# Block-sparse attention feeding a gated MLP: the ninth unit's scores and the fifth pair's loads moved behind the first stage, and the weight transfers issued by GpSimd instead of ScalarE

## The chip, the cores and the metric

One core of one Trainium2 chip. The metric is the device time of one execution in microseconds (us). The engines are named as in the profile: PE is TensorE (PEld its weight loads), DVE is VectorE, ACT is ScalarE, POOL is GpSimd, SP is SyncE; "ACTq" and "SPq" are rows for transfers that the sequencers of ACT and SP issue.

## The reference, cut to what matters

```python
# attention: q, k, v are (4 batches, 8 heads, 768 rows, 64); blocks of 32 rows, 24 blocks
scores = (q @ k^T) / 8
mask   = |block_i - block_j| <= 1, or either block is the first or last,
         or block_j is one of 3 sampled blocks of block_i
attn   = softmax(where(mask, scores, -1e9)) ;  out = attn @ v
# gated MLP over the 3072 rows of 512 numbers
h = x @ w_in ;  g = h * sigmoid(1.702 * h) ;  y = g @ w_out      # w_in 512x2048, w_out 2048x512
```

All in float32; w_in and w_out come as 64-bit words whose conversion to float32 is done on the chip.

## The kernel before

**Units, pairs and chunks.** The work on attention is cut into 48 units of 64 rows (two blocks of a batch). Two units of the same rows in two batches share their loads: such a pair has one entry in `kent` (keys, `load_k`: about ten transfers on SP, 1.5 MB) and one in `vent` (values, `load_v`: one or three on SP and two gathers of 512 KB each on POOL). There are two buffers for each (`RING`), so an entry's loads can go out when the entry two before it has been used. Eight units give the 512 rows of a chunk of the MLP; there are six chunks of 16 steps `m` (one slice of 128 hidden columns each), 96 steps in all.

**One unit** goes through `scores` (32 small matmuls, then on DVE four minima, L285, and on ACT four exponentials, L297), `transposes` (8 on PE, two copies L318 on ACT), `factors`, `values` (64 small matmuls), `normalise` (L381) and `turn` (transposes, then `xhi` on ACT L399 and `xlo` on DVE L400).

**One step of the MLP**, `tick(m)`: `up` (12 matmuls, L499 to L501, float32 in three products of high and low parts), `gate` (ACT L507 and L512, DVE L514), `gate_hi` (ACT L519), `gate_lo` (DVE L527), and `down` of the step before (12 matmuls, L545 to L550).

**The weights' conversion**, `weights`, is a generator of 32 items k, one for each slice of w_in or w_out in turn (k even from 2 on is w_out). Item k is fetched (L422: 512 KB of words into `raw`, 3 buffers), then ACT L430 makes `a` (3 buffers), DVE L454, L460 and L464 finish it, ACT L467 copies its high part and DVE L435 gives the low part; for w_out the finished `a` is also stored to `ws` (L441, 256 KB) for the later chunks. The fetch of item k+2 is called at the start of item k and reuses the buffer that L464 of item k-1 has read; the store of item k-1 is called right after that. The generator stops after each few instructions and is advanced by hand: 21 advances in the first stage, then nine in a step, or six in a step in which a unit's scores are due (`tick`, `heavy`).

**What sets the order.** Every engine runs its own list in program order, and the order is written by hand: `first` (the first stage: the first nine units, one after the other, with the first five weights) and then `plan`, which gives each further unit a place on a clock of four quarters per step. In `plan`, chunk 1's units begin at quarter -4, which puts the ninth unit's scores into `first`; `begin` calls `loads` at each quarter. In `first`, `vmost` holds back all value loads but the first until the second unit's minima are done: POOL copies `nm` to `seen` (L703), and later gathers stand behind that copy in POOL's list. Transfers on SP and ACT take their landing semaphores from one set of eight in turn (`DMAHW0` to `7`), those on POOL from another (`DMASW0` to `7`); the one that takes a semaphore again waits until the transfer that had it before has landed.

## Time and profile before

| what | us |
|---|---|
| median of 3 runs (785.55 to 786.63) | 786.6 |
| the profiled execution: its own time | 786.88 |
| its span, first to last instruction | 785.1 |
| first stage, up to the first matmul of `up` | 77.43 |
| chunk 0, 16 steps | 123.0 |
| PE busy | 739.7 (94%) |
| DVE busy | 412.9 (53%) |
| ACT busy | 383.4 (49%) |
| POOL busy | 45.8 (6%) |

1.8 us of the profiled execution lie outside its span. Matmuls of one PE overlap in the records, so PE's busy time is larger than its work; the pace of PE is read from the distance between the starts of like matmuls.

### The profile page before, as it was taken

How to read it: one execution, taken by the hardware profiler on the slowest of the kernel's cores; microseconds unless marked ns; L12 is line 12 of the kernel's file. 1: busy time of each engine (PE TensorE's matmuls, PEld its weight loads, DVE VectorE, ACT ScalarE, POOL GpSimd, SP SyncE). 2: the span in 40 equal slices, each digit the busy share in tenths (PEclk: the TensorE clock that was granted, in tenths of full speed). 3: DMA queues.
4: the chain of work that ended last, by engine and by line, in shares of the span. 5: the costliest groups of instructions: out<-in, count | busy, mean ns of one | idle time of the engine just before them, and what ended most of it. 6: DMA issues, size and time to landing. Idle time of an engine off the chain costs nothing.

```text
span 785.1 us, 19231 instructions
## 1 busy us (share of the span) xinstructions
PE 739.7 (94%) x7584; PEld 571.3 (73%) x7584; DVE 412.9 (53%) x1076; ACT 383.4 (49%) x951; POOL 45.8 (6%) x67
## 2 busy tenths in 40 slices
PE   2675999999999999999999999999999999999997
PEld 2453776767777777787787787787777777788885
DVE  4465888888554444554444445445454444443333
ACT  3455667766645444454444454544455445333232
POOL 3011011011000000000000000000000000000000
PEclk9787999999999999999999999999999999999999
DMA  8997887876664256563443564544574231131111
GB/s 246 293 336 255 271 277 234 257 247 225 205 187 162 75 168 188 168 204 115 150 147 110 163 187 121 156 128 126 171 249 156 68 108 41 41 96 52 47 47 55
DMA packets 62956, 128.21 MB, mean 163 GB/s; under 512 B 7569, under 2 KB 28946, under 8 KB 62354
## 3 DMA queue, kind: packets, MB, share of 16 engines
q1 hardware_dynamic: 48802, 82.08, 34.7%
q0 software_dynamic: 6336, 23.07, 8.7%
q10 hardware_dynamic: 7728, 21.84, 8.5%
q8 instruction: 60, 0.98, 0.5%
q14 instruction: 30, 0.25, 0.1%
HBM read 116.47 MB, written 10.49 MB: 162 GB/s over the span
## 4 chain that ended last, share of the span: by engine, by line
PE 77%; DMA 7%; DVE 7%; ACT 5%; issue 2%; SPq 1%; ACTq 0%; DVEq 0%
PE bank L499 11%; PE bank L549 10%; PE bank L550 10%; PE bank L545 10%; PE bank L501 10%; PE bank L500 10%; PE bank L313 5%; PE bank L339 4%; PE bank L262 4%; DMA ws<-a 2%; DMA vmid<-in_v_dram 2%; PE bank L347 2%; PE bank L274 2%; DVE a L460 1%; ACT ex L297 1%
## 5 line engine op out<-in xcount | busy, mean ns | idle before, releaser
L499 PE MATMUL bank<-xhi,win 128*128 128x512 f32 x384 | 158.2, 412 | 0.5 <-DVE g L514 0.2
L514 DVE SCALAR_TENSOR_TENSOR g<-g,bank 128x512 f32<-128x512 f32 x83 | 57.0, 687 | 184.3 <-ACT g L507 184.3
L549 PE MATMUL bank<-wout,ghi 128*128 128x512 f32 x384 | 153.9, 401 | 0.0
L550 PE MATMUL bank<-wout,ghi 128*128 128x512 f32 x384 | 152.0, 396 | 0.0
L501 PE MATMUL bank<-xhi,win 128*128 128x512 f32 x384 | 150.8, 393 | 0.0
L500 PE MATMUL bank<-xlo,win 128*128 128x512 f32 x384 | 150.6, 392 | 0.0
L297 ACT ACTIVATE ex<-bank,nm 128x256 f32<-128x256 f32 (+1 forms) x172 | 82.8, 490 | 116.7 <-DVE nm L285 116.5
L507 ACT ACTIVATE g<-bank 128x512 f32<-128x512 f32 x96 | 57.4, 598 | 146.7 <-PE bank L501 145.4
L545 PE MATMUL bank<-wout,glo 128*128 128x512 f32 x384 | 107.7, 394 | 0.0
L488 DVE TENSOR_TENSOR wout<-wst,wout 128x512 fp32r<-128x512 f32 x80 | 55.4, 692 | 79.7 <-ACT wout L487 78.7
L285 DVE CUSTOM_DVE_ANT_1 bank<-bank,bias 128x256 f32<-128x256 f32 x176 | 73.8, 440 | 23.2 <-PE bank L262 20.2
L499 PEld LDWEIGHTS bank<-xhi,win 128*128 128x128 f32 x384 | 72.1, 188 | 19.0 <-ACT wst L512 1.3
L519 ACT CAST ghi<-g 128x512 fp32r<-128x512 f32 x96 | 59.6, 621 | 53.1 <-DVE g L514 53.1
L545 PEld LDWEIGHTS bank<-wout,glo 128*128 128x128 f32 x384 | 72.1, 188 | 17.4
L550 PEld LDWEIGHTS bank<-wout,ghi 128*128 128x128 f32 x384 | 72.2, 188 | 16.5
L549 PEld LDWEIGHTS bank<-wout,ghi 128*128 128x128 f32 x384 | 72.1, 188 | 16.4
L501 PEld LDWEIGHTS bank<-xhi,win 128*128 128x128 f32 x384 | 72.1, 188 | 16.0
L500 PEld LDWEIGHTS bank<-xlo,win 128*128 128x128 f32 x384 | 72.2, 188 | 12.8
L262 PE MATMUL bank<-kg,qt 64*32 64x256 f32 x1408 | 54.9, 408 | 22.5 <-DMA kg<-in_kb_dram 18.6
L218 POOL DMA_INDIRECT vown<-in_v_dram,vidx x44 | 43.2, 983 | 516.7 <-PE bank L339 402.0
L318 ACT COPY pt<-bank 128x512 f32<-128x512 f32 (+1 forms) x112 | 56.9, 560 | 29.8 <-PE bank L313 29.6
L527 DVE TENSOR_TENSOR glo<-g,ghi 128x512 fp32r<-128x512 f32 x96 | 65.7, 685 | 0.7 <-ACT ghi L519 0.7
(88 smaller groups left out, 809.7 us busy)
## 6 DMA issues: line engine op xcount, KB each, us to landing
wst<-ws SPq DMA_DIRECT2D x80, 256.0 KB
kg<-in_kb_dram SPq DMA_DIRECT2D x151, 128.0 KB
kg<-in_kb_dram SPq DMA_DIRECT2D x22, 384.0 KB
raw<-in_moe_w_in_dram ACTq DMA_DIRECT2D x16, 512.0 KB
raw<-in_moe_w_out_dram ACTq DMA_DIRECT2D x16, 512.0 KB
kg<-in_kT_dram SPq DMA_DIRECT2D x4, 1536.0 KB
vown<-in_vd_dram SPq DMA_DIRECT2D x8, 768.0 KB
qt<-in_q_dram SPq DMA_DIRECT2D x22, 256.0 KB
```

The source lines that it names most:

```text
L262: nc.tensor.matmul(sps[h][BLK * c:BLK * (c + 1), n * i:n * (i + 1)].rearrange("p (n s) -> p n s", s=BLK), self.qt[r][rows, bi, UT * pair + ...
L285: nc.vector.tensor_tensor_reduce(out=at, in0=at, in1=bias, scale=-SCALE, scalar=3.0e38, op0=ALU.add, op1=ALU.min, accum_out=un["nm"][:, ha ...
L297: nc.scalar.activation(out=ex, in_=sps[h][:, n * k:n * (k + 1)], func=AF.Exp, bias=un["nm"][:, half, c:c + 1], scale=-1.0, accum_out=un["r ...
L499: nc.tensor.matmul(h, wih[:, k], hi[:, k], start=(k == 0), stop=False)
L500: nc.tensor.matmul(h, wih[:, k], lo[:, k], start=False, stop=False)
L501: nc.tensor.matmul(h, wil[:, k], hi[:, k], start=False, stop=(k == NCT - 1))
L507: nc.scalar.activation(out=g, in_=self.h, func=AF.Tanh, scale=0.851)
L519: self.nc.scalar.copy(out=ghi, in_=self.g[m][0])
L527: self.nc.vector.tensor_tensor(out=glo, in0=g, in1=ghi.bitcast(F32), op=ALU.subtract)
L545: nc.tensor.matmul(o[n], glo[:, tk[n]], woh, start=False, stop=last)
L549: nc.tensor.matmul(o[n], ghi[:, tk[n]], woh, start=(f == 0), stop=False)
L550: nc.tensor.matmul(o[n], ghi[:, tk[n]], wol, start=False, stop=False)
```

## The change

Three edits. `plan` begins chunk 1 at quarter 4 instead of -4, and `first` treats eight units and not nine, so the ninth unit's scores stand in the loop, and chunk 1's eight units are spread over 52 quarters from quarter 4 on (at 4, 10, 17, 23, 30, 36, 43, 49) where seven of them stood at 4, 12, 20, 28, 36, 44, 50. `kmost` and `vmost` hold back the entries of the fifth pair and later until the eighth unit's minima: `hold` puts the copy to `seen` into POOL's list, and a small transfer from `nm` to `seen` into SP's. And the transfers L422 and L441 are issued by POOL.

```diff
-        self.vmost = 1
+        self.kmost, self.vmost = CU // 2, 1
...
-            if self.knext < len(self.kent) and (self.knext < RING or not self.kent[self.knext - RING]["scores"]):
+            if self.knext < self.kmost and (self.knext < RING or not self.kent[self.knext - RING]["scores"]):
...
-                nc.scalar.dma_start(out=raw, in_=self.w64[i][f])
+                nc.gpsimd.dma_start(out=raw, in_=self.w64[i][f])
...
-                nc.scalar.dma_start(out=self.ws[f], in_=tiles[k]["a"].bitcast(F32))
+                nc.gpsimd.dma_start(out=self.ws[f], in_=tiles[k]["a"].bitcast(F32))
...
-            begin = -4 if c == 1 else 4 * QT * (4 * c - 4) - 8
+            begin = 4 if c == 1 else 4 * QT * (4 * c - 4) - 8
...
-        nc, items = self.nc, self.items[:CU + 1]
+        nc, items = self.nc, self.items[:CU]
...
+        def hold(g, k):
+
+            nc.gpsimd.tensor_copy(out=self.seen[:, 0:NPAIR], in_=g["unit"]["nm"][:, 0])
+            self.vmost = k
+
...
             if n == 1:
-                nc.gpsimd.tensor_copy(out=self.seen[:, 0:NPAIR], in_=g["unit"]["nm"][:, 0])
-                self.vmost = len(self.vent)
+                hold(g, CU // 2)
...
+        behind = self.transposes(items[CU - 1])
+        after = self.values(items[CU - 2])
+        finish(behind[:2])
+        finish(self.turn(items[CU - 3]))
+        finish(behind[2:])
+        finish(after)
+        weights(4)
+        after = self.values(items[CU - 1])
         finish(self.turn(items[CU - 2]))
-        finish(self.values(items[CU - 1]))
+        finish(after)
+        hold(items[CU - 1], len(self.vent))
+        nc.sync.dma_start(out=self.seen[:, NPAIR:2 * NPAIR], in_=items[CU - 1]["unit"]["nm"][:, 0])
+        self.kmost = len(self.kent)
+        self.loads()
         finish(self.turn(items[CU - 1]))
-        self.loads()
```

**ACT in the first stage**, at the eighth unit. The names: `ghi` and `glo` hold a unit's exponentials, `wst` and `pt` its transposed ones; a wait's name ends in a number that is the same for all. Before:

```order
L467 CAST wout_117<-a 128x512 [waits DVE_49]
L422 DMA raw<-in_moe_w_in_dram 128x1024 [waits DMAHW2_49,Activation_49]
L441 DMA ws_69<-a 128x512 [waits DMAHW5_49]
L430 ACTIVATE a<-raw 128x512 [waits DMAHW1_49,Activation_49]
L318 COPY wst<-bank_88 128x512 [waits PE_49]
```

In the changed kernel:

```order
L467 CAST wout_117<-a 128x512 [waits DVE_49]
L430 ACTIVATE a<-raw 128x512 [waits DMASW4_49,Activation_49]
L318 COPY wst<-bank_88 128x512 [waits PE_49]
L318 COPY wst<-bank_92 128x512 [waits PE_49]
L297 ACTIVATE ghi,rs<-bank_89,nm 128x256 [waits DVE_49]
```

The two issues with their waits for earlier landings no longer stand ahead of L430; L430 itself waits for its own words alone.

**POOL's list around the end of the first stage**, as a difference (`vown_97` and `vown_98` are the two buffers of gathered values, `ws_69` to `ws_71` the stored slices):

```order
+L441 DMA ws_69<-a 128x512
+L422 DMA raw<-in_moe_w_out_dram 128x1024
+L422 DMA raw<-in_moe_w_in_dram 128x1024
+L687 COPY seen<-nm 128x4
+L218 DMA vown_97<-in_v_dram,vidx 128x1024 x2
+L218 DMA vown_98<-in_v_dram,vidx 128x1024 x2
+L441 DMA ws_70<-a 128x512
+L422 DMA raw<-in_moe_w_out_dram 128x1024
+L422 DMA raw<-in_moe_w_in_dram 128x1024
+L441 DMA ws_71<-a 128x512
```

The four gathers of the fifth and sixth pair, which were two and two with the first stage's last third between them, stand together, and between the fetch of item 7 (the `w_in` row ahead of the copy) and the store `ws_70` of item 4, with the fetches of items 8 and 9 behind.

**ACT at the first two steps of the loop** (`g`, `wst` and `ghi` are the gate's; `ex` the exponentials of the unit whose scores stand at quarter 4). Before:

```order
L512 COPY wst<-bank_92 128x512
L422 DMA raw<-in_moe_w_out_dram 128x1024 [waits DMAHW6_49]
L430 ACTIVATE a<-raw 128x512 [waits DMAHW5_49,DMAHW3_49,Activation_49]
L519 CAST ghi<-g 128x512 [waits DVE_49]
L467 CAST wout_119<-a 128x512 [waits DVE_49]
```

In the changed kernel:

```order
L512 COPY wst<-bank_92 128x512
L430 ACTIVATE a<-raw 128x512 [waits DMASW0_49,DVE_49]
L519 CAST ghi<-g 128x512 [waits DVE_49]
L467 CAST wout_119<-a 128x512 [waits DVE_49]
L297 ACTIVATE ex,rs<-bank_85,nm 128x256 [waits DVE_49,PE_49]
...
L507 ACTIVATE g<-bank_92 128x512 [waits PE_49]
L512 COPY wst<-bank_92 128x512
L430 ACTIVATE a<-raw 128x512 [waits DMASW6_49,DMASW5_49]
```

L430 of item 7 waits for one transfer (its words) where it waited for two (the words and the store `ws_70`); the second landing, `DMASW5`, is now awaited by L430 of item 8.

## Rows read from the trace of the kernel before

**Rows 1.** The busy time of each engine in four stretches (us from the span's start: the stretch, its length, then PE, PEld, DVE, ACT and POOL busy with the count of instructions, the granted clock as a share, the DMA engines' busy share and GB/s): the end of the first stage in two parts, steps 0 and 1, and steps 2 to 15.

```profile
40.77:57.30 16.53, 13.54 (x318) 9.10 (x302) 12.10 (x39) 9.96 (x30) 2.15 (x3) 0.84 1.04 340
57.30:77.43 20.13, 8.77 (x183) 6.35 (x183) 10.98 (x36) 9.55 (x29) 3.28 (x4) 0.75 0.78 250
77.43:90.20 12.77, 12.34 (x145) 9.10 (x143) 10.12 (x25) 7.86 (x20) 0.19 (x1) 1.00 0.94 311
90.20:200.45 110.25, 106.82 (x1174) 81.69 (x1175) 93.96 (x222) 75.92 (x178) 9.37 (x8) 1.00 0.76 245
```

**Rows 2.** The matmuls of L499 alone (four to a step) in chunk 0, in chunk 3 with its eight units, and in thirteen steps without attention: stretch, length, PE and PEld busy with counts, clock, DMA share, GB/s.

```profile
77.43:200.45 123.02, 26.63 (x64) 12.16 (x65) 1.00 0.78 252
446.64:562.45 115.81, 26.58 (x65) 12.21 (x65) 1.00 0.52 155
693.38:765.76 72.38, 20.47 (x53) 9.75 (x52) 1.00 0.23 62
```

**Rows 3.** The chain of waits that ended last, from 53 us on: start, length, what.

```profile
53.55 7.37 DMA vmid<-in_v_dram
60.95 0.34 ACTq L441
...
61.39 0.66 ACT a L430
62.05 0.96 ACT wst L318 x2
63.01 0.92 ACT ghi L297 x4
63.93 0.91 ACT glo L297 x4
64.84 0.27 ACT xhi L399
...
77.78 5.35 DMA ws<-a
```

**Rows 4.** ACT in order of time: start, length, engine, line, operation, tiles, count, and in brackets the idle time before it with what ended it.

```profile
45.77 0.47 ACT L297 ACTIVATE ghi<-bank,nm 128x256 f32<-128x256 f32 x1 [0.73 <-DVE nm L285]
52.56 0.47 ACT L297 ACTIVATE ghi<-bank,nm 128x256 f32<-128x256 f32 x1
61.39 0.66 ACT L430 ACTIVATE a<-raw 128x512 f32<-128x512 f32 x1 [4.32 <-DMA vmid<-in_v_dram]
62.89 0.50 ACT L297 ACTIVATE ghi<-bank,nm 128x256 f32<-128x256 f32 x1
69.76 0.47 ACT L297 ACTIVATE ghi<-bank,nm 128x256 f32<-128x256 f32 x1 [0.48 <-DVE nm L285]
71.58 0.37 ACT L399 CAST xhi<-bank 128x256 fp32r<-128x256 f32 x1
83.23 0.67 ACT L430 ACTIVATE a<-raw 128x512 f32<-128x512 f32 x1 [1.69 <-DMA ws<-a]
90.04 0.70 ACT L430 ACTIVATE a<-raw 128x512 f32<-128x512 f32 x1
121.83 0.33 ACTq L441 DMA_DIRECT2D ws<-a  x1
126.48 0.68 ACT L430 ACTIVATE a<-raw 128x512 f32<-128x512 f32 x1 [1.14 <-DMA ws<-a]
```

**Rows 5.** DVE in order of time, columns as in rows 4: the ninth unit's first minimum and the end of item 4.

```profile
68.66 0.43 DVE L285 CUSTOM_DVE_ANT_1 bank<-bank,bias 128x256 f32<-128x256 f32 x1
72.93 0.68 DVE L464 SCALAR_TENSOR_TENSOR a<-raw,a 128x512 int32<-128x512 int32 x1
160.05 0.54 DVE L454 TENSOR_SCALAR a<-a 128x512 int32<-128x512 int32 x1
```

**Rows 6.** PE: the first matmul of step 0, a unit's scores, the first of steps 1 and 2 (columns as in rows 4).

```profile
77.43 0.48 PE L499 MATMUL bank<-xhi,win 128*128 128x512 f32 x1
80.36 1.09 PE L262 MATMUL bank<-kg,qt 64*32 64x256 f32 x32
90.22 0.50 PE L499 MATMUL bank<-xhi,win 128*128 128x512 f32 x1
```

**Rows 7.** POOL's gathers (columns as in rows 4), and over all 44 of them the time from issue to landing.

```profile
75.44 0.94 POOL L218 DMA_INDIRECT vown<-in_v_dram,vidx  x1 [16.24 <-PE bank L339]
76.68 0.94 POOL L218 DMA_INDIRECT vown<-in_v_dram,vidx  x1 [0.30 <-PE bank L392]
159.23 1.11 POOL L218 DMA_INDIRECT vown<-in_v_dram,vidx  x1 [27.32 <-PE bank L339]
...
DMA to landing us min/median/max: 4.5/6.1/9.6
```

**Rows 8.** ACT's waits from 57 to 192 us (who waited for whom: total us, times, longest), and over the whole span the durations of L454 (ns min/median/max, first and last start, form).

```profile
ACT a L430 <- DMA ws<-a: 5.9, 6, 1.7
...
L454 DVE TENSOR_SCALAR a<-a x32: 396/420/537, 36.2 to 189.3; 128x512 int32<-128x512 int32 x32
```

**Rows 9.** SP's issue of a pair's key loads (columns as in rows 4).

```profile
81.58 0.35 SPq L189 DMA_DIRECT2D qt<-in_q_dram  x1
83.76 6.29 SPq L200 DMA_DIRECT2D kg<-in_kb_dram  x6
```

More of the change, by code (lines that the diff above doesn't have):

```diff
@@ L671, in first @@
     def first(self):
-        nc, items = self.nc, self.items[:CU + 1]
-        assert items[CU]["unit"]["n"] == CU
+        nc, items = self.nc, self.items[:CU]
+        assert self.items[CU]["unit"]["n"] == CU
         nc.scalar.activation(out=self.seen[:, 0:1], in_=self.zero, func=AF.Exp)
@@ L683, in weights @@
                 next(self.conv)
+        def hold(g, k):
+            nc.gpsimd.tensor_copy(out=self.seen[:, 0:NPAIR], in_=g["unit"]["nm"][:, 0])
+            self.vmost = k
         for n, g in enumerate(items):
-            behind = []
-            if n == CU:
-                behind = self.transposes(items[n - 1])
             exps = self.scores(g)
-            if 0 < n < CU:
-                behind = self.transposes(items[n - 1])
+            behind = self.transposes(items[n - 1]) if n else []
             if n > 3:
```

## The prediction, made before the changed kernel ran

> **What bounds the kernel now.** I read the busy times by stretch first, then the distances of like matmuls, then the chain of waits, then ACT, DVE and POOL in order of time around the end of the first stage. In the last 20 us of the first stage no engine is near full: PE, DVE and ACT are busy 8.8, 11.0 and 9.6 of 20.1 us [rows 1]; engines wait for each other and for landings. In chunk 0 PE and DVE are both close to full: in steps 2 to 15, 110.25 us, DVE is busy 93.96, and PE shows 106.82 [rows 1]. How much PE could give is seen from like matmuls [rows 2]: thirteen steps without attention take 72.38 us, 5.57 each; chunk 3 with its eight units takes 115.8, so a unit costs PE (115.8 - 16 x 5.57) / 8 = 3.3 us. Seven units in chunk 0 would give 112 us, and it takes 123.0. From chunk 1 on the pace is PE's and the change touches nothing there, so only two numbers matter: when chunk 0 starts, and how long it lasts.
>
> Sums are made on the profiled execution (786.88 us, of which 785.1 are its span); the median of the runs, 786.6, is 0.3 less. About 0.2% (1.6 us) is what a measurement of this kernel can tell from no change.
>
> **The first stage gets shorter: the stall.** The chain [rows 3] goes from a value load (`vmid`, 53.55 to 60.9) through ACT's issue of a store (L441 at 60.95) to L430 at 61.39. ACT does not need that load; its store takes a landing semaphore that the load had, and ACT stood idle 4.32 us for it [rows 4]. With both issues on POOL this wait is POOL's. The eighth unit's exponentials, at 62.89, would then follow the seventh's (52.56) by the distance that the seventh's kept from the sixth's (45.77), 6.79 us: at 59.35. **Gain 3.5 us.** The words of items 0 and 1 go out some 10 us sooner, since POOL's list has nothing ahead of them that waits, while the second pair's keys are landing; item 2's words then stand behind two gathers on POOL. These pull both ways; I take 0, from a loss of 2 to a gain of 1.
>
> **The first stage gets shorter: the ninth unit.** Its minima start at 68.66 and xhi follows its exponentials at 71.58 [rows 4, 5], 2.9 us on the way from the eighth unit's exponentials to step 0. They go from here; the two copies of transposes and one L430, which fill part of this time today, stay on ACT. **Gain 2.5 us** (1.5 to 3). Step 0 would begin at 77.43 - 3.5 - 2.5 = 71.4 [rows 6].
>
> **The first stall of the loop.** L430 of item 7 waits at 83.23 for a store, 1.69 us [rows 4]. In the new order it waits only for its words and for DVE; the store is awaited by L430 of item 8, one step on. I take 1.5. So step 2, which began at 90.22 [rows 6], would begin 7.5 us sooner, at 82.7.
>
> **What POOL's list gives back.** Item 4's end (L464 at 72.93 [rows 5], 0.7 long) moves up by the stall's 3.5 and some 1.8 of the ninth unit's time, to 68.3. Only then can POOL issue item 7's words, which stand ahead of the copy and of four gathers; a gather takes 0.94 and 0.30 until the next [rows 7], so from about 69.9 to 74.9, and the store `ws_70` goes out at 75, item 8's words at 76.2. A gather lands 6.1 us after its issue at the median, 9.6 at the longest [rows 7], so item 8's words are there at 82.3 to 85.8. ACT would reach item 8's L430 at 90.04 - 7.5 = 82.5 [rows 4]. A wait of 0 to 3.3 us, and a shorter one at item 9. I take **2 us**, past the median, since just then both pairs' keys, 3 MB on SP, and 3.75 MB on POOL want to move within 20 us, some 340 GB/s, which is all that a stretch shows (340 GB/s at a share of 1.04 [rows 1]). The keys themselves have time: SP needs some 8.5 us for a pair [rows 9], from about 60 on, and the scores need them only at about 74.
>
> **The unit that moves into the loop.** From step 2 on, chunk 0 holds seven units' starts where it held six. One more costs PE 3.3 us [rows 2], DVE about as much. Both engines are used as densely as now, so I scale by the 123.0 us of chunk 0 over its 112 of PE's work, which gives 3.6, and take **3.5 us** (3.0 to 4). The scores alone, 1.09 us on PE [rows 6], are not the price, because the whole chain of units moves with them.
>
> **The transfers' latency.** A store issued by ACT at 121.83 frees its buffer for L430 at 126.48 [rows 4], 4.65 us. From POOL the fetch goes first (0.94 and 0.30), and a transfer of POOL lands after 4.5 to 9.6 us, 6.1 at the median [rows 7]: 5.7 to 10.8, at the median 7.3, so 2.7 us later. That price comes from gathers of twice the bytes; the change's plain transfers have no row. L430 stands seven advances behind the L464 that makes the store possible. In a step of nine advances that is some 5.5 us, in a step of six 8 or more. In the new order the whole distance lies within or almost within a nine-advance step for items 13, 21, 27 and 31 and partly for 17; a wait of 1.8 at four and 0.9 at one is 8.1 us, against 4.2 now (5.9 less the 1.69 [rows 4, 8]). Of the 4 us more, PE loses perhaps three quarters, since ACT's gates are queued behind the waiting L430 and PE's `down` behind the gates: **3 us**, from 0 (the latency is that of ACT's) to 7 (it binds at every pair of items).
>
> A figure of the Trainium skill would make this smaller: "DMA: Bandwidth & Descriptors", section Latency and other measured facts, gives a first byte after about 0.6 us from ACT or SP and about 1 us from POOL. By that alone the term would be near 0.5 us and the sum about -1.5. The rows here, in which POOL's transfers land 1.5 us later than ACT's store at the median, speak for more.
>
> **The sum:** -3.5 - 2.5 - 1.5 + 2 + 3.5 + 3 = **+1.0 us**, 786.6 + 1.0 = **787.6 us**: what the first stage gains, the loop gives back.
>
> **The rivals.**
>
> *A: the latency hides, faster.* If POOL's plain transfers land like ACT's, the last term is 0 and the wait at item 8 shrinks to 0.5: -7.5 + 0.5 + 3.5 = -3.5, **783 us**. For it: a plain transfer needs no list of rows, and POOL issues at L464's end, without ACT's queue ahead of it. Against it: the gathers' 6.1 us.
>
> *B: the store's landing becomes the loop's clock, slower.* The place is the chain L464 - POOL's fetch - store - landing - L430, three items long, in chunk 0. It decides where that distance passes the eight advances between two odd items' L430, some 8 us. Were it 9 (7.3, and 1.5 from L430 to the next L464), each of some eleven pairs from item 9 on would be 1 us late: 11 us less the 4 that ACT waits now, +7 where I took +3; with 3 at item 8 it gives +6 to +8, **794 us**. For it: six stores already end an idle time of ACT [rows 8], with the shorter latency. Against it: there is slack in steps of six.
>
> *C: DVE and POOL lock each other out, slower.* L454 begins right when L464 ends, and so does POOL's fetch. While a gather ran from 159.23, L454 took 0.54 where it takes 0.42 [rows 5, 7, 8]: 0.12 us, for 32 items at most 4 us. If the fetch held it up for its whole 0.94 us, 27 items in chunk 0 would cost up to 25 us of a DVE that is 85% busy, half of it seen: **800 us**. The Trainium skill says something like it ("SBUF — State Buffer", section Who interferes with whom): DVE's two-port modes and GpSimd shut each other out for a whole instruction. The 0.12 us of this trace speaks against the full price.
>
> *D: the first stage does not shrink.* If the early words delay the second pair's keys, or item 2's words come late behind the gathers, the 3.5 us shrink to 1: +3.5, **790 us**.
>
> **How the numbers follow.** Forecast 0.45, A 0.27, B 0.18, C 0.04, D 0.06. The forecast's own range is 784.5 to 791. A alone is faster; of the forecast's 0.45 some 0.08 are, 0.22 lie within 0.2% and 0.15 are slower; with B, C and D: faster 0.35, same 0.22, slower 0.43. The lower end takes all terms at their favourable bounds, -8.5 + 0 + 3.2 + 0: 781. The upper is B with 3 us of D: 796. C's tail is left out.
>
> **What would show it.** Right: the first matmul of step 0 at 71 to 72.5; no idle time of ACT at the eighth unit put down to `vmid`; POOL with four gathers in a row at about 70 to 75 and `ws_70` behind them; L430 of items 8 and 9 waiting for POOL's transfers; step 2 at 82 to 85; more ACT idle time put down to `ws` in chunk 0 than 5.9 us; the rest of the kernel, from chunk 1 on, as long as before. Wrong: a chunk 0 of less than 126 us from step 0 on (then A), or of more than 134 (then B or C, told apart by whether ACT's L430 waits or DVE's L454 is longer), or a step 0 at 74 or later (D).

## The result, and the profile after

| | before | changed |
|---|---|---|
| median, us (runs) | 786.6 (785.55 to 787.7, 4) | **797.4** (796.35 to 798.36, 4) |
| span of the profiled execution | 785.1 | 794.6 |
| first matmul of step 0 | 77.43 | 70.50 |
| chunk 0 | 123.04 | 139.46 |

The ratio is 1.0137, with a 95% interval of 1.0118 to 1.0156: 10.8 us slower. 787.6 was forecast, with 796 as the upper end. In the traces the first stage is 6.9 us shorter (6.0 forecast) and chunk 0 is 16.4 us longer; from chunk 1 on nothing differs (584.6 us in both). The profiled execution of the changed kernel was the fastest of its four, so the traces hold 9.5 of the 10.8 us.

The windows of the changed kernel (columns as in [rows 1]): the end of the first stage, steps 0, 1 and 2, and steps 2 to 15.

```profile
57.30:70.50 13.20, 8.00 (x211) 5.42 (x209) 8.27 (x26) 6.84 (x20) 2.68 (x6) 0.76 0.78 232
70.50:77.18 6.68, 6.58 (x45) 4.24 (x45) 3.94 (x8) 2.26 (x5) 4.20 (x5) 0.58 0.95 304
77.18:84.41 7.23, 6.90 (x33) 5.35 (x33) 5.93 (x16) 4.63 (x13) 1.40 (x3) 1.00 1.04 400
84.41:96.34 11.93, 9.98 (x121) 6.93 (x121) 8.79 (x22) 7.49 (x19) 1.27 (x3) 0.86 0.92 281
84.41:209.96 125.55, 114.95 (x1281) 86.75 (x1281) 97.24 (x233) 78.46 (x188) 27.32 (x43) 0.97 0.76 235
```

Some of these matmuls, in order of time (columns as in [rows 6]), the first two of steps 0 and 1:

```profile
70.50 0.80 PE L499 MATMUL bank<-xhi,win 128*128 128x512 f32 x1 [0.46 <-ACT xhi L399]
71.97 0.63 PE L499 MATMUL bank<-xhi,win 128*128 128x512 f32 x1
...
77.18 0.50 PE L499 MATMUL bank<-xhi,win 128*128 128x512 f32 x1
77.97 0.39 PE L499 MATMUL bank<-xhi,win 128*128 128x512 f32 x1
```

Against [rows 1] three things are new: step 0 runs at a granted clock of 0.58, for most of it the lower of the two levels (1.2 of 2.4 GHz), so that its second L499 comes 1.47 us behind the first where step 1 takes 0.79; the transfers of step 1 take the DMA engines' whole share (1.04 at 400 GB/s, where steps 0 and 1 had 0.94 at 311); and PE, which was busy 106.8 of 110.3 us in steps 2 to 15, is busy 115.0 of 125.6.

POOL at the end of the first stage, in order of time (columns as in [rows 7]):

```profile
68.65 0.20 POOL L687 COPY seen<-nm 128x4 f32<-128x4 f32 x1
69.02 1.01 POOL L218 DMA_INDIRECT vown<-in_v_dram,vidx  x1 [0.17 <-issue]
70.33 0.97 POOL L218 DMA_INDIRECT vown<-in_v_dram,vidx  x1 [0.30 <-PE bank L392]
71.60 1.31 POOL L218 DMA_INDIRECT vown<-in_v_dram,vidx  x1 [0.30 <-DVE wout L435]
73.22 0.94 POOL L218 DMA_INDIRECT vown<-in_v_dram,vidx  x1 [0.30 <-issue]
74.16 0.60 POOL L441 DMA_DIRECT2D ws<-a  x1
74.73 0.58 POOL L422 DMA_DIRECT2D raw<-in_moe_w_out_dram  x1
```

The backlog is the one that the prediction drew: four gathers, then `ws_70`, then item 8's words. ACT in order of time (columns as in [rows 4]), the eighth unit's first exponential and then the time of step 2:

```profile
58.84 0.47 ACT L297 ACTIVATE ghi<-bank,nm 128x256 f32<-128x256 f32 x1 [0.59 <-DVE nm L285]
...
85.41 0.66 ACT L430 ACTIVATE a<-raw 128x512 f32<-128x512 f32 x1 [1.06 <-DMA raw<-in_moe_w_out_dram]
88.18 0.67 ACT L430 ACTIVATE a<-raw 128x512 f32<-128x512 f32 x1 [1.08 <-DMA ws<-a]
88.76 1.05 ACT L318 COPY pt<-bank 128x512 f32<-128x512 f32 x2
```

Items 8 and 9 wait 2.1 us together. What the prediction did not have is the last row: the copies of the ninth unit's transposes stand behind item 9's L430, and the next unit's scores wait 1.95 us for them. The waits in chunk 0 (who waited for whom: total us, times, longest), and the landings of POOL's fetches L422:

```profile
PEld bank L262 <- ACT pt L318: 13.4, 12, 4.0
PE bank L262 <- ACT pt L318: 8.7, 6, 3.6
ACT a L430 <- DMA raw<-in_moe_w_out_dram: 3.9, 5, 1.3
ACT a L430 <- DMA ws<-a: 3.9, 4, 1.2
```
```profile
DMA to landing us min/median/max: 3.7/5.0/10.6
```

L262 are a unit's scores. In the loop `psum` gives scores and transposes the same banks 0 and 1, so a unit's scores cannot begin before ACT has copied its predecessor's transposes out of them (L318). ACT's own waits for stores, which rivals A and B turned on, went down from 5.9 us [rows 8] to 3.9.

**Where the 16.4 us lie.** The length of each step, from its first matmul L499 to the next one's, in the profiled execution of each kernel (us):

| kernel | step 0 begins | 0 | 1 | 2 | 3 to 7 | 8, 9 | 10, 11 | 12 to 15 | chunk 0 |
|---|---|---|---|---|---|---|---|---|---|
| before | 77.4 | 5.0 | 7.8 | 7.8 | 38.7 | 14.5 | 15.2 | 34.1 | 123.0 |
| **changed** | 70.5 | 6.7 | 7.2 | 11.9 | 39.4 | 21.4 | 14.5 | 38.2 | 139.5 |
| e1 | 74.0 | 5.0 | 6.7 | 7.8 | 38.5 | 15.3 | 15.2 | 34.1 | 122.6 |
| e2 | 74.2 | 6.7 | 9.0 | 9.5 | 40.3 | 21.1 | 14.6 | 38.2 | 139.3 |
| e3 | 75.5 | 4.9 | 7.8 | 7.1 | 40.8 | 14.6 | 17.0 | 34.6 | 126.8 |
| e4 | 70.1 | 6.6 | 7.7 | 7.8 | 40.1 | 19.5 | 15.7 | 38.0 | 135.3 |
| e5 | 70.3 | 4.4 | 7.2 | 15.4 | 38.5 | 20.9 | 14.6 | 38.0 | 139.1 |
| e6 | 70.4 | 6.8 | 7.1 | 11.9 | 40.5 | 21.3 | 14.5 | 39.1 | 141.2 |
| e7 | 75.7 | 5.0 | 6.7 | 8.8 | 42.4 | 22.0 | 14.6 | 31.6 | 131.0 |
| e8 | 75.5 | 5.7 | 6.7 | 7.8 | 37.6 | 14.6 | 16.4 | 33.0 | 121.9 |
| e9 | 71.5 | 5.8 | 7.2 | 11.1 | 42.5 | 19.1 | 14.6 | 38.4 | 138.7 |
| e10 | 72.5 | 6.5 | 7.2 | 8.1 | 44.1 | 20.0 | 14.5 | 40.4 | 140.9 |
| e11 | 70.0 | 5.5 | 6.6 | 11.1 | 40.9 | 19.1 | 16.0 | 36.8 | 136.0 |
| e12 | 72.4 | 5.8 | 7.2 | 11.6 | 39.8 | 22.5 | 14.5 | 37.9 | 139.4 |
| e13 | 70.8 | 6.0 | 7.2 | 10.5 | 40.6 | 20.8 | 14.5 | 37.8 | 137.4 |
| e14 | 77.4 | 6.2 | 6.7 | 7.9 | 40.9 | 22.0 | 14.5 | 32.3 | 130.5 |
| e15 | 73.5 | 6.7 | 7.2 | 7.9 | 40.6 | 22.8 | 14.5 | 38.9 | 138.7 |
| e16 | 76.9 | 4.6 | 7.9 | 6.7 | 38.8 | 14.7 | 23.0 | 31.6 | 127.3 |
| e17 | 70.8 | 6.6 | 7.2 | 12.0 | 37.9 | 19.7 | 14.5 | 34.7 | 132.5 |
| e18 | 74.0 | 5.0 | 6.7 | 7.8 | 35.6 | 14.5 | 14.5 | 31.3 | 115.3 |

The changed kernel loses in step 0 (1.7), in step 2 (4.1), in steps 8 and 9 (6.9) and in 12 to 15 (4.1). Each length is that of one execution, and an execution can lie some way off its kernel's median: e4's was 3.0 us below, e10's 3.9 above.

### The profile page after: what moved, and what is told of

Its sections match the earlier page's. It is cut to its first block, busy times and chain, and to the rows that moved or that the text cites. A ratio compares the mean times of both kernels' runs of the same rounds, so it can differ in the third digit from the quotient of the medians.

```text
span 794.6 us, 19264 instructions
## 1 busy us (share of the span) xinstructions
PE 748.6 (94%) x7584; PEld 575.8 (72%) x7584; DVE 413.6 (52%) x1076; ACT 383.1 (48%) x951; POOL 72.4 (9%) x116
## 3 DMA queue, kind: packets, MB, share of 16 engines
q0 software_dynamic: 12224, 44.05, 17.3%
## 4 chain that ended last, share of the span: by engine, by line
PE 77%; DMA 7%; ACT 6%; DVE 5%; issue 3%; SPq 2%; ACTq 0%; DVEq 0%; POOLq 0%
PE bank L499 11%; PE bank L549 10%; PE bank L550 10%; PE bank L501 10%; PE bank L500 10%; PE bank L545 10%; PE bank L313 5%; PE bank L339 4%; PE bank L262 4%; DMA kg<-in_kb_dram 2%; DMA ws<-a 2%; PE bank L347 2%; PE bank L274 2%; ACT ex L297 1%; DMA raw<-in_moe_w_out_dram 1%
## 5 line engine op out<-in xcount | busy, mean ns | idle before, releaser
L499 PE MATMUL bank<-xhi,win 128*128 128x512 f32 x384 | 159.5, 415 | 2.7 <-DVE g L514 1.5
L297 ACT ACTIVATE ex<-bank,nm 128x256 f32<-128x256 f32 (+1 forms) x176 | 84.8, 491 | 122.7 <-DVE nm L285 122.4
L499 PEld LDWEIGHTS bank<-xhi,win 128*128 128x128 f32 x384 | 72.8, 190 | 22.9 <-ACT wst L512 2.7
L262 PE MATMUL bank<-kg,qt 64*32 64x256 f32 x1408 | 58.7, 415 | 27.9 <-DMA kg<-in_kb_dram 18.3
L550 PEld LDWEIGHTS bank<-wout,ghi 128*128 128x128 f32 x384 | 72.2, 188 | 16.4
L549 PEld LDWEIGHTS bank<-wout,ghi 128*128 128x128 f32 x384 | 72.1, 188 | 16.4
L318 ACT COPY pt<-bank 128x512 f32<-128x512 f32 (+1 forms) x112 | 56.8, 559 | 25.4 <-PE bank L313 25.3
```

Source lines behind the costliest of these rows:

```text
L262: nc.tensor.matmul(sps[h][BLK * c:BLK * (c + 1), n * i:n * (i + 1)].rearrange("p (n s) -> p n s", s=BLK), self.qt[r][rows, bi, UT * pair + ...
L297: nc.scalar.activation(out=ex, in_=sps[h][:, n * k:n * (k + 1)], func=AF.Exp, bias=un["nm"][:, half, c:c + 1], scale=-1.0, accum_out=un["r ...
L499: nc.tensor.matmul(h, wih[:, k], hi[:, k], start=(k == 0), stop=False)
L549: nc.tensor.matmul(o[n], ghi[:, tk[n]], woh, start=(f == 0), stop=False)
L550: nc.tensor.matmul(o[n], ghi[:, tk[n]], wol, start=False, stop=False)
```

## The experiments

e1, e2 and so on are the first parts of the runs' labels. Theory 1, formed from the waits above: the loss comes from the units' new distances. Units at 4, 12, 20, ... have four quarters of a step between one unit's transposes and the next one's scores; at 4, 10, 17, 23, ... two or three. (The kernel before has two such distances of 6 as well, after its starts at 44 and 50.) Ratios are to the kernel before, each with its 95% interval.

### Which part of the change: e1, e2

**e1**, the kernel before with the two issues on POOL alone:

```diff
-                nc.scalar.dma_start(out=raw, in_=self.w64[i][f])
+                nc.gpsimd.dma_start(out=raw, in_=self.w64[i][f])
...
-                nc.scalar.dma_start(out=self.ws[f], in_=tiles[k]["a"].bitcast(F32))
+                nc.gpsimd.dma_start(out=self.ws[f], in_=tiles[k]["a"].bitcast(F32))
```

> The kernel before with the two issues on POOL and nothing else: nine units in the first stage, chunk 1's units at quarters 4, 12, 20, 28, 36, 44, 50. Theory 1 (what chunk 0 lost comes from the eight units at distances of 6 and 7 quarters: the scores of a unit need the two PSUM banks that its predecessor's transposes fill, and must wait until ACT has copied them, L318): no such waits here beyond those of the kernel before, the stall of ACT at the eighth unit goes, step 0 starts at 73 to 74 instead of 77.4, chunk 0 lasts 121 to 124, total 782 to 784. Rival 2 (POOL's issues make the weights late all through chunk 0): chunk 0 lasts 128 or more, total 788 to 792.

784.3 us, 0.998 (0.9965 to 0.9994): **faster** than both kernels, by 2 us against the one before. Chunk 0 takes 122.55 where it took 123.04, although L430 waits 6.5 us there for stores and waited 5.7 before. The transfers' latency, +3 in the prediction, costs chunk 0 nothing.

**e2**, the changed kernel with these two lines as before:

> The changed kernel with the two issues back on ACT: the ninth unit in the loop and the fifth pair's loads held back, as changed. Theory 1 (distances of units): chunk 0 keeps nearly all of its loss, 136 to 139 us from step 0 to step 16; step 0 at 70.5 to 73, the total 796 to 800. Rival 2 (POOL's issues): chunk 0 falls back to 126 to 128, total 786 to 789. Rival 3 (POOL's backlog of four gathers ahead of the words of items 8 and 9): only step 2 gets shorter, from 11.9 to about 9, total 794 to 795.

799.95 us, 1.0169 (1.0147 to 1.0191). All of chunk 0's loss is there without POOL's issues: 139.32. Rival 2 falls; the change's two halves pull apart, -2 and +13.7 us.

### One unit more, or closer units: e3, e7

**e3**, the changed kernel with `begin = 0` in place of 4: eight starts at 0, 8, 16, 24, 32, 38, 44, 50.

> The changed kernel with chunk 1's units from quarter 0 on instead of 4: they stand at 0, 8, 16, 24, 32, 38, 44, 50, so four of the seven distances are 8 again, and three are 6, like the last two of the kernel before. Same number of units in chunk 0, same issues on POOL. Theory 1: the waits of scores for L318 at steps 2 and 8 go, chunk 0 lasts 131 to 133 instead of 139.5, total 789 to 791. Rivals 2 and 3 (POOL's transfers or its backlog): nothing changes or it gets worse, since the weights are as late as before and the work starts sooner, 796 to 799.

789.1 us, 1.0028 (1.001 to 1.0046), chunk 0 126.75, steps 2 and 8 without their loss. Its loop holds eight units' starts, and its chunk 0 is 4.2 us longer than e1's with seven. That is not the price of a unit alone: the first of the eight stands ahead of step 0's first matmul, and three of the distances are 6 where e1 has one. So it does not contradict the prediction's 3.5 us, and does not show it either.

**e7**, e1 with its seven starts closer together and nothing else:

```diff
+                if c == 1:
+                    q = (-4, 4, 10, 17, 23, 30, 36, 43)[k] - begin
                 starts.append((begin + q, g))
```

> The kernel before with the two issues on POOL, nine units in the first stage and so seven starts in the loop as before, but those seven at the distances of the changed kernel: 4, 10, 17, 23, 30, 36, 43 instead of 4, 12, 20, 28, 36, 44, 50. The work in every stage stays that of the first experiment; only the distances change. Theory 1: the scores wait for L318 at steps 2 and 8 again, chunk 0 lasts 130 to 134 where that kernel's took 122.6, total 792 to 796. Rival 5 (what chunk 0 lost is the work of one unit more, in engines that are full): chunk 0 stays at 122 to 124, total 784 to 786.

793.7 us, 1.0087 (1.0068 to 1.0107). **With the same work as e1 chunk 0 takes 131.04, 8.5 us more**; steps 8 and 9 take 22.0 where e1 takes 15.3. Rival 5 falls: the distances alone make about half of the loss.

### What happens at step 8: e4, e9, e12, e14

PE and then ACT in the changed kernel at step 8 (columns as in [rows 4] and [rows 6]):

```profile
138.49 1.16 PE L313 MATMUL bank<-ident,ex 128*128 128x128 f32 x8
141.59 1.10 PE L545 MATMUL bank<-wout,glo 128*128 128x512 f32 x4
146.28 1.58 PE L262 MATMUL bank<-kg,qt 64*32 64x256 f32 x32 [3.60 <-ACT pt L318]
```
```profile
138.83 0.62 ACT L519 CAST ghi<-g 128x512 fp32r<-128x512 f32 x1
139.34 0.69 ACT L430 ACTIVATE a<-raw 128x512 f32<-128x512 f32 x1
139.92 0.61 ACT L467 CAST wout<-a 128x512 fp32r<-128x512 f32 x1
141.12 0.68 ACT L430 ACTIVATE a<-raw 128x512 f32<-128x512 f32 x1 [0.58 <-DMA raw<-in_moe_w_out_dram]
143.05 0.62 ACT L467 CAST win<-a 128x512 fp32r<-128x512 f32 x1 [1.26 <-DVE a L464]
143.57 0.59 ACT L507 ACTIVATE g<-bank 128x512 f32<-128x512 f32 x1
144.06 0.58 ACT L512 COPY wst<-bank 128x512 f32<-128x512 f32 x1
145.09 0.67 ACT L430 ACTIVATE a<-raw 128x512 f32<-128x512 f32 x1 [0.45 <-DMA ws<-a]
145.67 1.05 ACT L318 COPY pt<-bank 128x512 f32<-128x512 f32 x2
```

The unit that starts at quarter 30 has its transposes at 34, in the third quarter of step 8. PE is through with them at 139.65, and has two quarters of work left, up to 142.7. ACT's copies stand in its list behind six advances of the weights and the gate, and come at 145.67. At the old places (scores at the first quarter of a step, transposes at the first of the next) the copies stand ahead of a step's weights, and PE has four quarters.

**e4**: transposes three quarters after the scores instead of four, so one quarter more for the copies.

```diff
-                turn = q + (4 if self.sparse(g) else 2)
+                turn = q + ((3 if q < 4 * QT * 4 - 8 else 4) if self.sparse(g) else 2)
```

> The changed kernel with the transposes of chunk 1's units three quarters after their scores instead of four, starts unchanged (4, 10, 17, ...): ACT has one quarter more (some 1.4 us of PE) for the copies before the next unit's scores want the banks. Theory 1: the scores' waits for L318 (22 us on PE and its weight loads in chunk 0) shrink by more than half, chunk 0 lasts 131 to 135, total 789 to 793; some of it comes back as waits of transposes for the exponentials L297. Rivals 2 and 3: no change, 796 to 798.

794.8 us, 1.0116 (1.0098 to 1.0135), chunk 0 135.31. Step 2 takes 7.79, what it takes in e1; step 8 still 11.5. PE's waits of scores for L318 fell from 8.7 to 1.9 us, and 3.0 came back as waits for exponentials. The median is above the expected range by 2 us.

**e9**: copies before the advances that lie behind the gate.

```diff
-            self.gate(m, lambda: run(n1))
-        finish(after[:2])
+            self.gate(m, lambda: (finish(after[:2]), run(n1)))
```

> The changed kernel with one order changed in the loop: where a unit's transposes or scores stand in the third quarter of a step, ACT's copies L318 (or exponentials L297) come before the three advances of the weights behind the gate, and so before an L430 that waits for a store to land, instead of after them. Theory 1 (the scores wait for the banks because the copies stand in ACT's list behind the weights): in step 2 the copies need not wait for item 9's L430 at 88.18, the scores' wait of 1.95 there goes and step 2 takes 8 to 9.5 instead of 11.9; in step 8, where the copies still stand behind two other items, 12 to 13 instead of 14.2; total 791 to 794. If ACT's order has no part in it (the weights themselves come late for `up` and `down`): 796 to 799.

798.5 us, 1.0157 (1.0137 to 1.0178). The expectation was wrong on step 2: the L430 of 88.18 belongs to the end of step 1's weights, and the edit does not move it. Step 8 did fall to 12.5, but steps 3 to 7 took 3.1 us more: an L430 waited 2.8 us for a store there, and PE waited 1.7 and 1.0 us for the gate's copy L512 behind it. No gain.

**e12** asks whether the shared banks carry the loss.

```diff
-..., {"s": (0, 1), "t": (0, 1), "a": (2,)}[what]
+..., {"s": (0, 1), "t": (5, 6) if k < 2 * CU else (0, 1), "a": (2,)}[what]
...
-        o = [self.bank[3 + n] for n in range(NN)]
+        o = [self.bank[3 + (n % 2 if c == 0 else n)] for n in range(NN)]
```

> The changed kernel with banks 5 and 6 for the transposes of chunk 0's units, so that scores (banks 0 and 1) never wait for the copies L318. To have the two banks, chunk 0's `down` adds the third and fourth block of tokens onto the first and second (same matmuls, same count; the results of the first 512 rows are mixed up). Theory 1 (the shared banks carry the loss): no scores wait for L318, chunk 0 falls from 139.5 to 127 to 131 us (the changed kernel from quarter 0 on took 126.8), total 785 to 789. Rival 6 (the weights' chain on ACT and DVE is the clock, the banks only show where PE waits for it): PE waits elsewhere, chunk 0 stays at 136 to 140, total 794 to 798.

799.9 us, 1.0169 (1.0148 to 1.0189), chunk 0 139.4: **theory 1 falls in the form in which the banks are the cause.** PE's waits in its chunk 0:

```profile
PE bank L339 <- DVE xlo L400: 6.4, 4, 4.3
...
PE bank L339 <- ACT pt L318: 1.8, 1, 1.8
PE bank L262 <- ACT pt L318: 1.4, 1, 1.4
```

With banks to spare the scores go ahead, and PE waits at the next row of its list, the values L339, for the same copies and for `xlo`, which follows them on ACT and DVE and frees the bank of the values. At step 8 the copies come 6.1 us behind PE's transposes, 6.0 in the changed kernel: the shared bank was only the first thing that met the late copies.

**e14**, the same two lines on e7:

> The kernel of e7 (nine units in the first stage, POOL's issues, seven starts at 4, 10, 17, 23, 30, 36, 43) with transposes in banks 5 and 6 in chunk 0 as in e12. Theory 1: the 8.5 us that the distances cost go, chunk 0 122 to 125 (e7 131.0, at distances of 8 122.6), total 784.5 to 787. Rival 6: 129 to 131, total 792 to 794.

795.5 us, 1.0111 (1.0094 to 1.0128), chunk 0 130.50, step 8 14.6: the same answer.

### Are the weights the cause: e13, e15, e16, e17, e18

**e13** leaves out the stores (`save` only drops the item, `stream` loads from `vd`).

> The changed kernel without the sixteen stores L441: later chunks load as many bytes of values instead of the stored slices, so w_out is wrong from chunk 1 on. No L430 waits for a store to land, POOL issues sixteen transfers less and 4 MB less are moved in the first 200 us. Theory 1: of the three waits of L430 that push copies (1.08, 0.45, 1.2 us) two go, chunk 0 136 to 138.5, total 794 to 796.5. Rival 6 in the form that the landing of stores is the clock of the weights' chain: chunk 0 128 to 132, total 786 to 790.

794.9 us, 1.0118 (1.0098 to 1.0138), chunk 0 137.4: two of the 16.4 us. **e15**, with e12's edit too:

> The edits of e12 and e13 together. If banks and stores each carry a part: 2 to 4 us less than e12 alone. If the banks carry all: as e12, within 1 us. If the stores do: as e13.

797.3 us, 1.0127 (1.0105 to 1.0149), chunk 0 138.7, more than with e13's edit alone: the two do not add.

**e16**: e7's edit with the starts 6, 14, 22, 30, 38, 44, 50.

> The kernel of e1 (nine units in the first stage, POOL's issues) with the seven starts at 6, 14, 22, 30, 38, 44, 50 instead of 4, 12, 20, 28, 36, 44, 50: the first five stand in the third quarter of a step instead of the first, at distances of 8. Theory 7 (ACT comes to a unit's copies some 7 us after PE's transposes when they stand in the third quarter, behind the weights and the gate; two quarters of PE's work, 2.8 us, don't cover that, four quarters, 5.6 us, nearly do): chunk 0 123 to 127, total 784 to 789. If the quarter alone makes the loss, whatever the distance: chunk 0 130 or more, total 792 or more.

788.3 us, 1.0031 (1.0013 to 1.0049). Through step 9 the transposes stand in the third quarter too, but at distances of 8, and nothing is lost (steps 8 and 9: 14.7). At 38 and 44 the distance falls to 6, the transposes are at 42, the scores at 44, and step 10 alone takes 15.65. PE and ACT there:

```profile
153.25 0.66 PE L313 MATMUL bank<-ident,ex 128*128 128x128 f32 x4 [0.26 <-ACT ex L297]
155.84 1.10 PE L545 MATMUL bank<-wout,glo 128*128 128x512 f32 x4
160.77 2.65 PE L262 MATMUL bank<-kg,qt 64*32 64x256 f32 x32 [3.83 <-ACT pt L318]
```
```profile
156.91 0.62 ACT L467 CAST win<-a 128x512 fp32r<-128x512 f32 x1 [2.12 <-DVE a L464]
159.05 0.67 ACT L430 ACTIVATE a<-raw 128x512 f32<-128x512 f32 x1 [0.55 <-DMA ws<-a]
160.14 1.07 ACT L318 COPY pt<-bank 128x512 f32<-128x512 f32 x2
```

So the place alone costs little. **Transposes in the third quarter with scores two quarters later** cost 5 to 7 us in three kernels: 14.15 in the changed one, 15.33 in e7 and 15.65 here, where 5.57 and a whole unit's 3.3 [rows 2] would be 8.9. Part of it is paid after the wait: the scores took 1.58 to 2.65 behind it, 1.09 without one [rows 6].

Place and distance together are not enough, though. e3 has the very same pair at step 10 (starts at 38 and 44), and that step takes 10.34. PE and then ACT there:

```profile
157.76 1.78 PE L262 MATMUL bank<-kg,qt 64*32 64x256 f32 x32 [0.27 <-ACT pt L318]
```
```profile
157.12 1.08 ACT L318 COPY pt<-bank 128x512 f32<-128x512 f32 x2
```

ACT had already done two of the weights' rows when PE's transposes ended at 154.5; four were left ahead of the copies, which came after 2.7 us. In the three expensive steps it was six, with two or three waits among them, and 6.0 to 6.3 us. The start at 50 gives the kernel before such a pair at step 13, which takes 9.8. The rows suggest that it matters how far ACT is behind PE at that moment, and the order alone does not fix that.

**e17** and **e18** leave L454 and L460 out, of the changed kernel and of e1:

> The changed kernel without two of the weights' three DVE instructions before the last (L454 and L460, about 1.0 us of DVE per item; the weights' values are wrong). Theory 7: with DVE a quarter less busy in chunk 0 (some 80 us instead of 107), ACT's L467 no longer waits for DVE and the copies come to their turn in time: chunk 0 falls from 139.5 to 119 to 126, total 777 to 784. If the weights on ACT and DVE are not what holds the copies up: chunk 0 134 or more.

> The same two instructions left out of the kernel of e1 (plan of before, POOL's issues). PE's own work for seven units is 112 us; theory 7: chunk 0 falls from 122.6 to 113 to 117, total 775 to 779, and the distance to e17 is 5 to 9 us where e1's to the changed kernel is 17. If the gap stays at 15 or more, the weights are not its cause.

790.3 us (1.0068, 1.0047 to 1.0089) and 775.9 us (0.9882, 0.9865 to 0.99). Chunk 0 of both, first e17 and then e18 (columns as in [rows 1]):

```profile
70.72:203.26 132.54, 125.49 (x1356) 95.80 (x1357) 81.40 (x202) 84.39 (x205) 31.75 (x50) 0.95 0.79 258
```
```profile
74.08:189.36 115.28, 115.28 (x1319) 90.49 (x1318) 77.88 (x191) 82.95 (x197) 28.80 (x47) 1.00 0.83 269
```

Both gain 7 us, and the gap between the two plans stays: 17.3 where it was 16.9. Theory 7 had put e17's chunk 0 at 119 to 126 and the gap at 5 to 9, and missed both: DVE's load is not the gap's cause. With DVE relieved the old plan runs at PE's pace, PE busy from end to end; the new one still loses 3.9 in step 8 (5.3 before the edit), where ACT's list puts another wait in front of the copies, this time for words. ACT in e17 at step 8:

```profile
140.10 0.66 ACT L430 ACTIVATE a<-raw 128x512 f32<-128x512 f32 x1 [1.75 <-DMA raw<-in_moe_w_out_dram]
142.69 1.07 ACT L318 COPY pt<-bank 128x512 f32<-128x512 f32 x2
```

So ACT's list is where step 8 loses its time; that its order alone does it is not shown, since e9 changed a part of the order without a gain in all, and e3 passes step 10 with the same pair of places.

### The other two losses: e5, e6, e10, e11

**e5**: thirteen matmuls in the gap ahead of step 0.

```diff
+    def warm(self, k):
+        for _ in range(k):
+            self.nc.tensor.matmul(self.bank[0], self.win[0][:, 0:P], self.win[0][:, 0:DM], start=True, stop=True)
...
         weights(4)
+        self.warm(4)
         after = self.values(items[CU - 1])
+        self.warm(3)
         finish(self.turn(items[CU - 2]))
+        self.warm(6)
```

> The changed kernel with thirteen matmuls more at the end of the first stage, on the first weight slice and into a bank that is free there (their product is not used): four before the last unit's values, three behind them, six before its last transposes, where PE idles now at a granted clock of 0.50 and then runs step 0 at 0.58. Theory 4 (part of the loss is that PE idles before step 0 and so runs it at the lower clock): step 0 still begins at 70.5 to 71.3, the first twelve matmuls of `up` stand 0.23 us apart instead of 0.43, step 0 lasts 4.3 to 5.2 instead of 6.7, total 795 to 796. If the clock stays down, or the thirteen only delay the last unit, 797 to 799.

796.0 us, 1.012 (1.0097 to 1.0143). Its windows just before step 0 and in it, and then ACT:

```profile
66.00:70.37 4.37, 3.29 (x33) 2.16 (x22) 2.78 (x7) 1.41 (x4) 1.74 (x4) 1.00 0.70 222
70.37:74.78 4.41, 4.27 (x45) 2.66 (x45) 3.94 (x8) 2.26 (x5) 3.80 (x5) 1.00 0.87 255
```
```profile
85.86 0.66 ACT L430 ACTIVATE a<-raw 128x512 f32<-128x512 f32 x1 [4.00 <-DMA raw<-in_moe_w_out_dram]
```

The clock stays up and step 0 is 2.3 us shorter. Then item 8's L430 waits 4.0 us for its words instead of 1.06, starts at 85.86, no sooner than in the changed kernel (85.41), and step 3 begins at 97.4 instead of 96.3. The clock was lost time, but not on the path.

**e6**: only two gathers ahead of those words (`hold(items[CU - 1], CU // 2 + 1)`, the rest after step 1).

> The changed kernel with only the fifth pair's two gathers at the end of the first stage; the sixth pair's two follow after step 1, so that ws_70 and the words of items 8 and 9 have two gathers less ahead of them in POOL's list (2.5 us sooner). Rival 3 (the backlog is the loss of step 2): ACT's waits at L430 of items 8 and 9 (1.06 and 1.08) go, step 2 falls from 11.9 to 8 or 9, and the total by 3 to 794. Theory 1 (the banks): the copies L318 behind those two L430 come up to 2 us sooner, so step 2 falls to 10 to 11, while steps 8, 12 and 13 stay: total 795 to 796.5. No change, 797, if the backlog hides altogether.

796.1 us, 1.0114 (1.0093 to 1.0134), step 2 11.9 as before the edit: item 8's words were in time, but item 9's L430 waited 2.24 for the store `ws_71`, which landed 8.6 us after its issue. POOL's list was not the whole of it; the transfers crowd each other.

**e10**: without the two holds (`kmost` from the start at its full length, `vmost` after the second unit's minima).

> The changed kernel without the two holds: the fifth pair's keys and values may go out as soon as their buffers are free, as in the kernel before; the ninth unit stays in the loop and POOL issues. Rival 3 in its second form (at step 2 the transfers of keys, values and words crowd each other, and land 7 to 10 us after their issue instead of 4 to 5): the crowd is gone, the words and stores that L430 of items 8 and 9 waits for land in time, step 2 takes 8.8 to 9.5 instead of 11.9 and the total is 794 to 796, if step 0 is not more than 1 us later. Steps 8, 12 and 13 stay as in the changed kernel by theory 1. If the holds cost nothing: step 2 stays at 11 to 12, total 797.

796.0 us, 1.0109 (1.0091 to 1.0127), and step 2 takes 8.1: the crowd is made by the held loads. In the profiled execution, though, steps 7 and 12 took 12.1 and 13.7 (8.9 and 10.1 in the changed kernel), again with scores waiting for L318. That execution was the slowest of six (799.9); the median gains 1.4. **e11**, the edits of e4, e5 and e9 together:

> Three of the edits together on the changed kernel: the transposes a quarter earlier, the copies before the weights in the third quarter, and the thirteen matmuls more ahead of step 0. If the losses are the three that theories 1 and 4 name and they add up: step 0 takes 4.4 (6.7), step 2 7.8 to 9 (11.9), step 8 10 to 12 (14.2), chunk 0 129 to 133 us instead of 139.5, total 786 to 791. If the gains replace each other (the words of item 8 land at a fixed time, about 85): chunk 0 135 or more, total 792 to 795.

794.3 us, 1.01 (1.0085 to 1.0114), chunk 0 136.0: the gains replace each other. Item 8's L430 again starts no sooner than 85.5, after 3.9 us of waiting for its words.

**e8**, as e7 with the starts 4, 12, 20, 28, 35, 42, 49:

> As the last, but with the starts at 4, 12, 20, 28, 35, 42, 49: three distances of 7 in place of 8, 8 and 6 at the end. Theory 1: two wide distances are given for a narrow one; what 44 and 50 lost at steps 12 and 13 (9.75 each, where a step with a unit's whole work needs 8.9) comes back in part, total 782.5 to 784, against 784.3 for the first experiment. If a distance of 7 costs as much as one of 6, 786 to 788.

784.7 us, 0.998 (0.9966 to 0.9995): not to be told from e1. Three distances of 7 cost no more here than two of 8 and one of 6.

Open stays why a wait that is taken away in an early step comes back in a later one (e9, e10); a run with the copies ahead of all weights of their step was not made. The first stage scatters too: kernels with e1's first stage began step 0 at 74.0 to 77.4, so a single profile does not carry its last 3 us.

## Why the prediction was wrong

**Right: the first stage.** Step 0 was to begin at 71.4 and began at 70.50; e1 alone brought 3.4 us of it (3.5 forecast) and e2 alone 3.2 (2.5), though kernels with e1's first stage scatter by 3 us, as said above. The eighth unit's exponentials came at 58.84 (59.35 forecast, 62.89 before [rows 4]), with no wait for `vmid`. Rival D falls. Item 7's L430 began at 77.01 without a wait, as forecast, but step 1 is only 0.6 us shorter, not 1.5.

**Right in place, short in size: POOL's backlog.** Item 8's words landed at 85.3 (82.3 to 85.8 forecast), and ACT waited 2.1 us at items 8 and 9 (2 forecast). But step 2 lost 4.1, since the ninth unit's copies stood behind the second of these waits. e10, whose step 2 takes 8.1, shows the held loads as the source.

**Wrong: the latency.** The term was +3 and measured -0.5 (e1 against before) and +0.1 (changed against e2). POOL's plain transfers land after 5.0 us at the median, not after a gather's 6.1 [rows 7], and L430's waits for stores, which the prediction put 4 us higher, came to 6.5 us in e1 (5.7 before) without lengthening chunk 0, and to 3.9 in the changed kernel. The estimate of near 0.5 from the first-byte figures of the Trainium skill, "DMA: Bandwidth & Descriptors", section Latency and other measured facts, was the better guide: e1's chunk 0 is not longer. Rivals B and C, at 794 and 800, lie on either side of the result, and both fall. B falls with the term. For C, L454 took 419 ns at the median, 420 before [rows 8]; of the nine that ran beside an instruction of POOL two were longer (508 and 599 ns). The Trainium skill's lock between DVE's two-port modes and GpSimd ("SBUF — State Buffer", section Who interferes with whom) could show in these two at most, some 0.3 us. The prediction had read a chunk 0 of more than 134 as B or C; it came for neither reason.

**The step that failed** is "The unit that moves into the loop": "Both engines are used as densely as now, so I scale by the 123.0 us of chunk 0 over its 112 of PE's work". The new starts stood in the description of the change, and the term priced them like the old ones. Moving the unit cut the distances from mostly 8 to 6 and 7, put transposes into the third quarter of a step, and left two quarters until the scores that need ACT's copies. That costs 8.5 us by itself (e7), where the term had 3.5 for everything. A part of the loss at step 8 could have been worked out beforehand: ACT's seven rows between `ghi` and the copies in the changed order, at some 0.55 each, are 3.9 us, against the 2.8 us that two quarters give. Most of the rest of PE's 3.6 us of waiting comes from ACT's own waits (0.58, 1.26 and 0.45), which the order does not show.

The term's other side, the work itself, was counted wrongly as well. The scores' matmuls L262 in chunk 0 and chunk 3 of the kernel before, and then in chunk 0 of the changed kernel (columns as in [rows 2]):

```profile
77.43:200.46 123.03, 10.91 (x288) 4.89 (x288) 1.00 0.78 252
446.64:562.45 115.81, 8.75 (x256) 3.90 (x256) 1.00 0.52 155
```
```profile
70.50:209.96 139.46, 15.17 (x320) 6.25 (x320) 0.96 0.78 246
```

At 32 to a unit, chunk 0 of the kernel before held nine units' scores, not the seven reckoned with, and one unit's more than chunk 3: the first two units of chunk 2 are scored before step 16's first matmul. So its floor on PE was not 112 us but about the 115.3 that e18 takes. And what the change brought in is one unit's scores and its eight transposes: PE's instructions in chunk 0 go from 1319 [rows 1] to 1359, and the values L339 are 576 in both, since the ninth unit's stood in the loop already. So "the whole chain of units moves with them" fails too: the scores' 1.09 us and some 1.1 for the transposes moved, not 3.3.

**Not seen at all:** without the ninth unit PE idles ahead of step 0, and `up` runs at the lower clock (granted 0.58), 1.7 us; e5 shows it off the path.

In sum, from e1's 122.6 us to e7's 131.0 it is 8.5 (distances). From e7 to the changed kernel's 139.5 it is 8.4, for the moved unit and the held loads together: 6.7 in steps 12 to 15, where the last unit now stands, 3.1 in step 2, 1.7 in step 0 and 0.6 in step 1, less 3.6 in steps 3 to 9. This second half is split by the table alone. e10, without the held loads, gets step 2 back, but its profiled execution loses as much in steps 3 to 7 and 12, so what the unit and the loads cost each stays open.

## What to carry to other kernels

A price per unit read from evenly spaced rows holds for that spacing alone: when a change packs units closer, count for each hand-over how much work the first engine has until it needs the result back, how many rows stand ahead of the answer on the other engine's list, and how far that engine is behind. A wait names the first thing that met a late result, so giving it a resource of its own (e12) tells whether the resource or the lateness is the cause. A change of several edits should be priced edit by edit: here one half is worth -2 us and the other +14.

## What the runs showed of the hardware

A fetch issued by POOL keeps it busy 0.53 us and lands after 5.0 us at the median (3.7 to 10.6), like the 256 KB stores (5.0); in the changed kernel's crowded stretch, issued from 69 to 80 us at a DMA share of 0.95 to 1.04, transfers of POOL and SP alike took 7 to 11 us. Thirteen matmuls at the end of the first stage held the granted clock at 1.00 in the 4.4 us ahead of step 0 and in step 0 itself, where without them it was 0.50 and 0.58.
